# Remainder queries of two heads in two column tiles, whole-block output stores, a new opening and a written-out engine order in a fused attention and maxout kernel

## The chip, the cores and the metric

The kernel runs on one core of one Trainium2 chip. The metric is device time in microseconds (us) of one execution; a "run" below is several executions of one kernel on one chip, with executions of the kernel before among them. The profiled execution of a run has a span that is about 2 us shorter than its time, since the span counts from the first to the last instruction.

Engine names as the profile has them: PE is TensorE (PEld its weight loads), DVE is VectorE, ACT is ScalarE, POOL is GpSimd, SP the engine that issues most transfers. "L582" is line 582 of the kernel in question; the same statement has another line number in another kernel, so lines are named in words too.

## The reference, cut to what matters

```python
q, k, v: (8 batches, 8 heads, 1152, 64)
q_pool = q.reshape(B, H, 576, 2, 64).mean(axis=3)          # 576 queries per head
attn   = softmax(q_pool @ k.T / 8)                          # 576 x 1152
x      = (attn @ v), heads side by side                     # 4608 tokens x 512
out    = maximum(x @ w1, x @ w2) @ w_out                    # 512 -> 1024 -> 512
```

The kernel uses max(a, b) = max(a - b, 0) + b. It therefore makes a hidden layer h = relu(x (w1 - w2)) and an output p = h w_out + x (w2 w_out). Two heads form a pair; there are 32 pairs, four to a batch. Per pair the kernel makes scores, exponentials and attention outputs (AV). Per batch it transposes the outputs (xT) for the hidden layer.

Of the kernel before, what the change touches and what calls it, by code (L numbers as in the profile page):

```python
# [7 lines left out]
P = 128  # L8
# [4 lines left out]
ALU = mybir.AluOpType  # L13


class Plan:
# [29 lines left out]
    def when(self, eng, r=(), w=(), after=()):  # L46

        t = self.free.get(eng, 0.0)
        for d in self.deps(r, w, after)[0]:
            p = self.ops[d]  # L50
            if p["eng"] != eng or p["dma"] is not None:
                t = max(t, p["seen"] + 0.05)
        return t

    def op(self, eng, fn, r=(), w=(), dma=None, cost=0.1, mode="f", after=(), solo=False):
# [9 lines left out]
        if dma is not None:  # L65
            self.free[eng] = t + (1.3 if mode == "t" else 0.5)
            self.dma_free = max(self.free[eng] + 1.2, self.dma_free) + cost
            seen = self.dma_free + 0.7
        else:
            if eng == "PE" and mode != self.mode:  # L70
                t += 0.1
                self.mode = mode
            self.free[eng] = t + cost
            seen = t + cost + self.LAT[eng]
# [8 lines left out]

    def solve(self):
# [3 lines left out]
        for n, o in enumerate(ops):  # L88
# [3 lines left out]
            for d in sorted(o["deps"], reverse=True):  # L92
                p = ops[d]
                if p["dma"] is None:
                    if p["eng"] == eng and (eng == "PE" or d not in o["raw"]):
                        continue
# [57 lines left out]
def bass_funnel_attn__then__act_maxout2_kernel(  # L154
# [32 lines left out]
    with ctx:  # L187
# [10 lines left out]
        qp = [sbuf([HP, QU, 2, D], BF16, f"qp{s}") for s in range(2)]  # L198
# [4 lines left out]
        et = sbuf([P, 4 * PW + HP], BF16, "et")  # L203
        et2 = et[:, 0:4 * PW].rearrange("p (h c) -> p h c", h=2)
# [25 lines left out]

        def setup():
# [5 lines left out]
            def ones(g):  # L237
                g.memset(et[:, 4 * PW:], 0.0)
# [4 lines left out]
            op("POOL", ones, w=["vE0", "vE1", "vE2", "pad"])  # L243

        def load_k(i, lo=0, hi=NT):
            b, h0, s = i // NHP, 2 * (i % NHP), i % 3
            op("SP", lambda e: e.dma_start(
                kraw[s][:, :, lo:hi, :],
                k[b, h0:h0 + 2, :, :].rearrange("h (p t) d -> p h t d", t=NT)[:, :, lo:hi, :]),
                w=[f"kraw{s}"] if hi == NT else [f"kraw{s}.0"], dma=f"d_k{s}" if hi == NT else "d_k",  # L250
                cost=1.5 * (hi - lo) / NT)

        def load_q(i):
            b, h0, s = i // NHP, 2 * (i % NHP), i % 3
            for half in range(2) if i == 0 else (None,):
                at = slice(0, P) if half is None else rows(half)
                hs = slice(h0, h0 + 2) if half is None else slice(h0 + half, h0 + half + 1)
                op("SP", lambda e, at=at, hs=hs: e.dma_start(
                    qraw[s][at, :, :, :].rearrange("p u r d -> p (u r d)"),
                    q[b, hs, :, :].rearrange("h (p r) d -> (h p) (r d)", p=HP)),  # L260
                    w=["qraw0.0"] if half == 0 else [f"qraw{s}"],
                    dma="d_q" if half == 0 else f"d_q{s}", cost=1.45 if half is None else 0.75)
# [8 lines left out]
        def cast_k(i):  # L271
# [4 lines left out]
                w=[f"kbf{s}"] + (["kbf0.0", "kbf0.3"] if i == 2 else []), cost=1.13)  # L276

        def cast_k0(lo, hi, part):
            op("ACT", lambda e: e.activation(
                kbf[0][:, lo:hi, :, :].rearrange("p t h d -> p h t d"), kraw[0][:, :, lo:hi, :],  # L280
                COPY), r=[part], w=[f"kbf0.{lo}"], cost=0.2 + (hi - lo) * 0.092)
# [10 lines left out]

        def cast_q(i):
            s, r = i % 2, i % 3
            for half in range(2):
                a = qraw[r][rows(half), :, :, :]
                op("DVE" if i == 0 else "POOL", lambda g, half=half, a=a: g.tensor_tensor(  # L297
                    qp[s][:, :, half, :], a[:, :, 0, :], a[:, :, 1, :], ALU.add),
                    r=["qraw0.0" if i == 0 and half == 0 else f"qraw{r}"], w=[f"qp{s}.{half}"], cost=0.65 if i == 0 else 1.4,
                    solo=i > 0 and half == 1)  # L300

        def cast_v(i):
# [3 lines left out]
                1.0, 1.0, ALU.mult, ALU.mult), r=[f"vraw{r}"], w=[f"vE{r}"], cost=1.13)  # L306

        def unit(r, cost, go, mode="f"):
# [3 lines left out]
            return r, plan_it, cost  # L312
# [4 lines left out]
        def qtrans(i):  # L317
# [10 lines left out]
            def evac(m):  # L328
                mb = fb[m][:, :].bitcast(BF16)
                dve(lambda e: e.tensor_copy(qpT[i % 3][:, :], mb[:, 0:SQ]),  # L330
                    [f"f{m}"], [f"qpT{i % 3}", f"f{m}"], 0.4)
            return Job("q", [unit([f"qp{s}.0", f"qp{s}.1", "ident"], 0.3, go, "s")], evac, ("q", i))

# [7 lines left out]
        def ktrans_pe(i, cuts=(0, 5, 9)):  # L341
# [3 lines left out]
            for lo, hi in zip(cuts, cuts[1:]):  # L345
# [8 lines left out]
                def evac(m, lo=lo, hi=hi):  # L354
# [4 lines left out]
                        [f"f{m}"], kkeys(i, lo, hi) + [f"f{m}"], 0.1 + (hi - lo) * 0.12)  # L359
# [5 lines left out]
        def av_jobs(i):  # L365
# [5 lines left out]
            need = [f"et{es}.{g - first(i)}" for g in range(first(i), after(i))] + [f"vE{vs}", "pad"]  # L371

            def chunk(half, sb):

                def go(e, m):
                    for t in range(NT):
                        a = (half * 2 + es) * PW + t * SQ + sb * P
# [5 lines left out]

            def norm(half):
                def evac(m):
                    c = c0 + half * D
                    a = fb[m][:, 0:(NCH + 1) * 66].rearrange("p (j c) -> p j c", c=66)
                    dve(lambda e: e.reciprocal(rc[half][:, :], a[:, :, 64:65]),  # L388
                        [f"f{m}"], [f"rc{half}"], 0.19)
                    dve(lambda e: e.tensor_tensor(  # L390
                        xnat[xs][:, :, c:c + D], a[:, :, 0:D],
                        rc[half][:, :].unsqueeze(2).to_broadcast([P, NCH + 1, D]), ALU.mult),
                        [f"f{m}", f"rc{half}"],
                        [f"xn{xs}.{h0 + half}", f"f{m}"], 0.5)
                return evac

            return [Job("a", [chunk(half, sb) for sb in range(NCH + 1)], norm(half), nb=i)
                    for half in range(2)]
# [21 lines left out]
        def skeys(g):  # L420
            return [key for i, t, *_ in pieces(g) for key in (f"kT{i % 3}.{t}", f"qpT{i % 3}")]

        def scores(g):
# [10 lines left out]
            def exp(a, z, keys):  # L434
# [3 lines left out]
                    r=[f"s{r}"], w=keys + [f"s{r}"], cost=0.24 + (z - a) / 700.0)  # L438
# [20 lines left out]
        def under(n0, n1):  # L459

            keys = [key for key, lo, hi in (("w2b", 512, 1536), ("w2T", 1536, 2560),
                                            ("w2f", 2560, NTOK)) if n0 < hi and lo < n1]
            if "w2T" in keys:
                keys += [f"w2T{ct}" for ct in range(NC_)]
            return keys

        def xsize(j):
            return P if j < NCH else NB

        def xtrans(b):  # L470
            xs = b % 2
            assert b == 0 or not queue["w"]
            for j in range(NCH + 1):
# [3 lines left out]
                    r=[f"xn{xs}.{h}" for h in range(H)], w=xkeys(n0, n0 + n),  # L477
                    after=under(n0, n0 + n), dma=f"d_x{xs}{j}", cost=0.65, mode="t")

        def xtrans_pe(b):  # L480
            xs = b % 2
            jobs = []
            for j in range(NCH + 1):
# [14 lines left out]
                jobs.append(Job("x", [unit([f"xn{xs}.{h}" for h in range(H)] + ["ident"],  # L498
# [15 lines left out]
        def w_cast(part, ct):  # L514
            if part == 0:
                dve(lambda e: e.tensor_copy(w2b[:, ct, :], w2f[:, ct, :]),
                    [f"w2f{ct}"], [f"w2b{ct}", "w2b"], 0.6)
            elif part == 1:
                dve(lambda e: e.tensor_tensor(  # L519
                    wd[:, ct, :], w1f[:, ct, :], w2f[:, ct, :], ALU.subtract),  # L520
                    [f"w1f{ct}", f"w2f{ct}"], [f"wd{ct}", "w2f"], 1.2)
            else:
                dve(lambda e: e.tensor_copy(  # L523
                    wo[:, 2 * ct:2 * ct + 2, :], wof[:, 2 * ct:2 * ct + 2, :]),
                    [f"wof{ct}"], [f"wo{2 * ct}", f"wo{2 * ct + 1}"], 0.6)

        def w2t_job(ct):
# [7 lines left out]
            def evac(m):  # L535
# [3 lines left out]
                    [f"f{m}"], [f"w2T{ct}", "w2T", f"f{m}"], 1.15)  # L539
            return Job("w", [unit([f"w2b{ct}", "w2b", "ident"], 0.44, go)], evac)  # L540
# [19 lines left out]
        def store(lo, s):  # L560

            for half in range(2):
                n0 = lo + half * HP
                b, at = n0 // SQ, n0 % SQ
                if b % 2:
                    at = (at - NB) % SQ
                op("SP", lambda e, b=b, u=at // HP, half=half: e.dma_start(
                    out[b * SQ:(b + 1) * SQ, :].rearrange("(p u) e -> u p e", u=QU)[u, :, :],
                    osb[s][rows(half), :]), r=[f"osb{s}"], dma=f"d_o{s}", cost=0.4)
# [4 lines left out]
        def h_jobs(nb, tail):  # L574
# [4 lines left out]
            for ft in range(NF):  # L579
# [6 lines left out]
                def evac(m, ft=ft):  # L586
# [5 lines left out]
                    else:  # L592
                        dve(lambda e: e.tensor_scalar_max(  # L593
                            gT[:, ft, g0:g0 + size], fb[m][:, 0:size], 0.0),
                            [f"f{m}"], w, 0.1 + size / 960.0)
# [3 lines left out]
        def p_job(lo, tail):  # L599
            hi = lo + P  # L600

            def part(j):
                def go(e, m):
# [5 lines left out]
                    return e.matmul(fb[m][:, :], lhs, rhs, start=(j == 0), stop=(j == NC_ + NF - 1))  # L609
                if j < NC_:  # L610
                    return unit([f"w21{j}"] + xkeys(lo, hi), 0.216, go)
                return unit([f"wo{j - NC_}", f"gT.{lo % RING // P}.{j - NC_}"], 0.216, go)

            def evac(m):
                o = ocount[0] % 4
# [6 lines left out]
                else:  # L622
                    dve(lambda e: e.tensor_copy(osb[o][:, :], fb[m][:, :]),  # L623
                        [f"f{m}"], [f"osb{o}", f"f{m}"], 0.63)
                held[o] = (lo, o)
            return Job("p", [part(j) for j in range(NC_ + NF)], evac, nb=hi)
# [11 lines left out]
        p_got = set()  # L638
        p_at = [0]
# [53 lines left out]
        def start_w(n):  # L693
            for ct in range(NC_):
                load("w", (n, ct), got_w, f"{('w2f', 'w1f', 'wof')[n]}{ct}")

        def got_w(at):
# [3 lines left out]
            def ready():  # L701
# [3 lines left out]
                elif n == 2 and ct == NC_ - 1:  # L705
# [18 lines left out]
        def flush():  # L724
# [24 lines left out]
            for b in list(x_wait):  # L749
# [3 lines left out]
                elif plan.ops[plan.writer[f"xn{b % 2}.{H - 1}"]]["seen"] <= now():  # L753
# [15 lines left out]
        def burst_size():  # L769

            done = [b for b in range(B) if all(av_half.get(b * NHP + j) == 2 for j in range(NHP))]
            return 3 if len(done) * SQ - p_end[0] > LAG else 2

        def more_moe():
# [10 lines left out]
            while p_at[0] + P <= h_end[0] and f"w21{NC_ - 1}" in plan.writer:  # L785
                queue["p"].append(p_job(p_at[0], tail))
# [58 lines left out]
        def emit_unit(kk):  # L845
# [17 lines left out]
            elif job.kind == "p":  # L863
                p_got.add(job.nb)
                while p_end[0] + P in p_got:
                    p_end[0] += P
            if job.done:
# [7 lines left out]

        setup()
        load_q(0)
        load_k(0, 0, 3)
        load_k(0, 3, NT)
        cast_k0(0, 3, "kraw0.0")  # L880
        cast_q(0)
        cast_k0(3, NT, "kraw0")
        queue["q"].append(qtrans(0))
        queue["k"].extend(ktrans_pe(0, (0, 3, NT)))
        load_k(1)
        load_q(1)
        load_v(0)
        cast_k(1)
        queue["k"].extend(ktrans_pe(1))
        cast_q(1)  # L890
        queue["q"].append(qtrans(1))
        cast_v(0)
        load("k", 2, load_k, "kraw2")
# [99 lines left out]
```

## The kernel before: what the change and the argument touch

A Python planner with a cost model decides the order of all engines at build time and greedily. Scores come in bursts, because the score matmuls use 64 rows of the array (both heads at once, in two row tiles) and nearly everything else uses 128, and going from one shape to the other costs time (95 to 99 ns in the trace of the kernel before). Each score group of 512 columns for both heads fills one of three buffers of 128x1024 f32 that TensorE writes, and ScalarE turns it into exponentials.

The AV of one head is five chunks of nine matmuls (576 queries are 4.5 blocks of 128, so the fifth chunk is half empty):

```python
def chunk(half, sb):
    def go(e, m):
        for t in range(NT):                                   # NT = 9
            a = (half * 2 + es) * PW + t * SQ + sb * P
            last = e.matmul(fb[m][:, sb * 66:sb * 66 + 65], et[:, a:a + P],
                            vE[vs][:, t, half, 0:65], start=(t == 0), stop=(t == NT - 1))
        return last
    return unit(need, 0.275, go)
...
return [Job("a", [chunk(half, sb) for sb in range(NCH + 1)], norm(half), nb=i) for half in range(2)]
```

An output block of 128 tokens goes out as two transfers of 64 rows. The 64 rows of a half lie 9 rows apart in the output, and the other half fills the rows next to them:

```python
def store(lo, s):
    for half in range(2):
        n0 = lo + half * HP                                   # HP = 64
        b, at = n0 // SQ, n0 % SQ
        if b % 2:
            at = (at - NB) % SQ
        op("SP", lambda e, b=b, u=at // HP, half=half: e.dma_start(
            out[b * SQ:(b + 1) * SQ, :].rearrange("(p u) e -> u p e", u=QU)[u, :, :],
            osb[s][rows(half), :]), r=[f"osb{s}"], dma=f"d_o{s}", cost=0.4)
```

The burst rule and the ranks of the greedy planner:

```python
return 3 if len(done) * SQ - p_end[0] > LAG else 2            # score groups in one burst
rank = {"q": 6, "k": 6, "x": 5, "a": 4, "w": 3, "p": 2, "h": 1}
```

The softmax here doesn't subtract the row's maximum and nothing guards it: scores larger than these inputs give would overflow.

## Time and profile before

The median was 384.99 us (383.74 to 385.46).

The first fence is the profile page of the kernel before: span, busy time by engine (share of the span, number of instructions), and rows of 40 equal slices of the span in tenths. PEclk is the granted TensorE clock.

```profile
span 382.8 us, 11318 instructions
...
PE 363.7 (95%) x5010; PEld 210.8 (55%) x5010; DVE 140.2 (37%) x283; ACT 316.9 (83%) x355; POOL 162.0 (42%) x135
...
PE   2787999999999999999999999999999999999995
...
ACT  3998989999999999999999999999899999902210
...
PEclk9999999999999999999999999999999999999999
...
DMA packets 93521, 88.58 MB, mean 231 GB/s; under 512 B 66080, under 2 KB 66592, under 8 KB 93472
```

The table by windows of the kernel before: for each stretch its length and the busy time (and instructions) of PE, PEld, DVE, ACT and POOL, then clock, DMA share and GB/s.

```profile
80.00:120.00 40.00, 39.94 (x575) 22.50 (x572) 13.10 (x28) 37.66 (x42) 19.92 (x17) 1.00 1.10 268
200.00:240.00 40.00, 40.00 (x584) 23.49 (x583) 13.47 (x28) 37.44 (x43) 18.33 (x16) 1.00 1.11 254
```

TensorE is busy all the time, ScalarE nearly so (37.4 to 37.7 of 40 us), and the last exponential ends at about 335 us while TensorE still has some 45 us of hidden layer and output to do.

I also split TensorE's time by the starts of the matmuls in the trace. "Streaming" is the pace of a dense row of them (29 ns for a 65-column matmul, 216 ns for 512). "Changes" is the extra time, up to 100 ns each (95 to 99 ns where nothing was waited for), where two neighbours use the array in different shapes (64-row transposes count as another shape than the scores; without that it is 261 changes, the prediction's "about 260"). "Waits" is the rest. A second count of this table, with slightly other paces, agrees to about 1 us in each row.

| kernel before, us | |
|---|---|
| before the first matmul | 6.7 |
| streaming | 325.5 |
| changes of shape (277) | 25.1 |
| waits (13.0 of them before 60 us) | 21.0 |
| last matmul's start to the end | 4.5 |

### The profile page before, as it was taken

The numbers are of one execution on the slowest core, as the hardware profiler recorded it, in microseconds if no ns is written. First come the engines' busy times: TensorE is split into PE (matmuls) and PEld (weight loads), VectorE is DVE, ScalarE is ACT, GpSimd is POOL, SyncE is SP. The second block draws the span as 40 slices with busy tenths as digits, with TensorE's granted clock in tenths as the row PEclk, the third lists the DMA queues.
The fourth block names the chain that finished last, engine by engine and source line by source line (L and its number), as shares of the span: only waits on it lengthen the run. The fifth ranks groups of instructions, "written<-read, shape, count | busy, mean of one in ns | idle before, by whom it ended". The sixth has DMA issues, their size and how long they took to land.

```text
span 382.8 us, 11318 instructions
## 1 busy us (share of the span) xinstructions
PE 363.7 (95%) x5010; PEld 210.8 (55%) x5010; DVE 140.2 (37%) x283; ACT 316.9 (83%) x355; POOL 162.0 (42%) x135
## 2 busy tenths in 40 slices
PE   2787999999999999999999999999999999999995
PEld 1365546555555555455556565555455655667642
DVE  2274934442234223422252224422442244237201
ACT  3998989999999999999999999999899999902210
POOL 1955597665554555555453535545545110000000
PEclk9999999999999999999999999999999999999999
DMA  8999999999989998999799999999899460121144
GB/s 248 405 391 399 392 257 312 331 309 312 225 234 295 273 272 174 309 320 275 142 265 289 319 179 212 286 258 315 200 236 267 94 109 14 29 44 42 29 95 98
DMA packets 93521, 88.58 MB, mean 231 GB/s; under 512 B 66080, under 2 KB 66592, under 8 KB 93472
## 3 DMA queue, kind: packets, MB, share of 16 engines
q1 hardware_dynamic: 93472, 87.86, 89.4%
q8 instruction: 39, 0.64, 0.7%
q14 instruction: 10, 0.08, 0.1%
HBM read 62.91 MB, written 9.44 MB: 189 GB/s over the span
## 4 chain that ended last, share of the span: by engine, by line
PE 85%; DMA 6%; DVE 4%; POOL 2%; issue 1%; SPq 1%; POOLq 0%
PE fb L378 22%; PE fb L609 21%; PE sps L429 18%; PE fb L582 15%; PE sps L609 4%; DMA qraw<-in_q_dram 3%; DMA kraw<-in_k_dram 2%; PE sps L582 2%; DVE wd L519 2%; POOL qp L297 1%; PE fb L547 1%; DVE xnat L390 1%; POOL vE L304 1%; PE fb L489 1%; DVE wo L523 1%
## 5 line engine op out<-in xcount | busy, mean ns | idle before, releaser
L436 ACT ACTIVATE et<-sps 128x1024 bf16<-128x1024 f32 (+1 forms) x336 | 307.8, 1005 | 19.0 <-PE sps L429 17.2
L378 PEld LDWEIGHTS fb<-vE,et 128*128 128x128 bf16 x2880 | 93.4, 97 | 20.9 <-issue 10.9
L378 PE MATMUL fb<-vE,et 128*128 128x65 bf16 x2880 | 101.9, 193 | 0.3
L297 POOL TENSOR_TENSOR qp<-qraw 64x576 bf16<-64x576 f32 x62 | 88.6, 1429 | 30.6 <-DMA qpT<-qp 21.3
L429 PE MATMUL sps<-qpT,kT 64*128 64x512 bf16 (+7 forms) x1152 | 96.9, 289 | 3.0 <-ACT et L436 2.1
L304 POOL TENSOR_SCALAR vE<-vraw 128x1152 bf16<-128x1152 f32 x32 | 36.9, 1152 | 103.2 <-PE fb L378 95.8
L429 PEld LDWEIGHTS sps<-qpT,kT 64*128 64x128 bf16 x1152 | 41.8, 95 | 51.3 <-issue 19.6
L582 PE MATMUL fb<-xT,wd 128*128 128x512 bf16 (+3 forms) x276 | 63.1, 360 | 0.7 <-DVE stage L623 0.7
L609 PE MATMUL fb<-wo,stage 128*128 128x512 bf16 x240 | 62.4, 380 | 0.0
L593 DVE TENSOR_SCALAR stage<-fb 128x512 bf16<-128x512 f32 (+3 forms) x64 | 41.9, 657 | 32.3 <-PE fb L582 32.1
L388 DVE RECIPROCAL rc<-fb 128x5 f32<-128x5 f32 x64 | 12.4, 194 | 112.3 <-PE fb L378 112.3
L273 POOL TENSOR_SCALAR kbf<-kraw 128x1152 bf16<-128x1152 f32 x31 | 36.2, 1167 | 14.6 <-DMA kraw<-in_k_dram 12.5
L582 PEld LDWEIGHTS fb<-xT,wd 128*128 128x128 bf16 x276 | 22.8, 98 | 29.4 <-DVE stage L593 6.3
L623 DVE COPY stage<-fb 128x512 f32<-128x512 f32 x29 | 20.0, 690 | 50.2 <-PE fb L609 49.7
L609 PEld LDWEIGHTS fb<-wo,stage 128*128 128x128 bf16 x240 | 21.1, 97 | 23.3 <-issue 3.3
L390 DVE TENSOR_TENSOR xnat<-fb,rc 128x320 bf16<-128x320 f32 x64 | 31.5, 491 | 2.2
L609 PE MATMUL fb<-w,xT 128*128 128x512 bf16 x120 | 32.1, 380 | 0.0
L609 PEld LDWEIGHTS fb<-w,xT 128*128 128x128 bf16 x120 | 10.3, 98 | 11.7 <-issue 2.0
L589 ACT ACTIVATE stage<-sps 128x256 bf16<-128x256 f32 (+1 forms) x7 | 2.3, 338 | 16.4 <-PE sps L582 16.4
L620 ACT COPY stage<-sps 128x512 f32<-128x512 f32 x3 | 1.8, 585 | 13.8 <-PE sps L609 13.8
L609 PE MATMUL sps<-wo,stage 128*128 128x512 bf16 x48 | 11.3, 379 | 0.0
L582 PE MATMUL sps<-xT,wd 128*128 128x256 bf16 (+2 forms) x76 | 10.3, 275 | 0.0
(40 smaller groups left out, 96.4 us busy)
## 6 DMA issues: line engine op xcount, KB each, us to landing
vraw<-in_v_dram SPq DMA_DIRECT2D x32, 576.0 KB, 7.7
kraw<-in_k_dram SPq DMA_DIRECT2D x31, 576.0 KB, 6.6
qraw<-in_q_dram SPq DMA_DIRECT2D x31, 576.0 KB, 5.8
out_dram<-stage SPq DMA_DIRECT2D x72, 128.0 KB, 2.4
xT<-in_moe_w_dram SPq DMA_DIRECT2D x4, 512.0 KB, 11.9
stage<-in_moe_w_out_dram SPq DMA_DIRECT2D x4, 512.0 KB, 14.2
stage<-in_moe_w_dram SPq DMA_DIRECT2D x4, 512.0 KB, 13.2
qraw<-in_q_dram SPq DMA_DIRECT2D x2, 288.0 KB, 4.1
```

What stands on the lines that cost most here:

```text
L273: op("POOL", lambda g: g.tensor_scalar(kbf[s][:, :, :, :].rearrange("p t h d -> p h t d"), kraw[r][:, :, :, :], 1.0, 1.0, ALU.mult, ALU.mu ...
L297: op("DVE" if i == 0 else "POOL", lambda g, half=half, a=a: g.tensor_tensor(qp[s][:, :, half, :], a[:, :, 0, :], a[:, :, 1, :], ALU.add), ...
L304: op("POOL", lambda g: g.tensor_scalar(vE[r][:, :, :, 0:D].rearrange("p t h d -> p h t d"), vraw[r][:, :, :, :], 1.0, 1.0, ALU.mult, ALU.m ...
L378: last = e.matmul(fb[m][:, sb * 66:sb * 66 + 65], et[:, a:a + P], vE[vs][:, t, half, 0:65], start=(t == 0), stop=(t == NT - 1))
L388: dve(lambda e: e.reciprocal(rc[half][:, :], a[:, :, 64:65]), [f"f{m}"], [f"rc{half}"], 0.19)
L390: dve(lambda e: e.tensor_tensor(xnat[xs][:, :, c:c + D], a[:, :, 0:D], rc[half][:, :].unsqueeze(2).to_broadcast([P, NCH + 1, D]), ALU.mult ...
L429: last = e.matmul(sps[r][:, h, col:col + hi - lo], kT[i % 3][rows(h), t, :], qpT[i % 3][rows(h), lo:hi], start=True, stop=True)
L436: op("ACT", lambda e: e.activation(et2[:, :, c:c + z - a], sps[r][:, :, a - g * W:z - g * W], EXP, scale=scale), r=[f"s{r}"], w=keys + [f" ...
L582: return e.matmul(fb[m][:, 0:size], wd[:, ct, ft * P:(ft + 1) * P], xT[:, ct, n0:n1], start=(ct == 0), stop=(ct == NC_ - 1))
L593: dve(lambda e: e.tensor_scalar_max(gT[:, ft, g0:g0 + size], fb[m][:, 0:size], 0.0), [f"f{m}"], w, 0.1 + size / 960.0)
L609: return e.matmul(fb[m][:, :], lhs, rhs, start=(j == 0), stop=(j == NC_ + NF - 1))
L623: dve(lambda e: e.tensor_copy(osb[o][:, :], fb[m][:, :]), [f"f{m}"], [f"osb{o}", f"f{m}"], 0.63)
```

## The change

Its intent: make the half-empty fifth chunks of a pair's two heads in one go, each head in one 64-column tile of the array; start earlier; make longer score bursts; store a block in one transfer; split the last block so that its store starts earlier; and replace the planner's greedy order on TensorE and VectorE by a table that was annealed on a model of the engines. The diff, cut to its core:

```diff
+ORDER = {"PE": ("000210000010110201000110000304400021200010000120011000300000201104...  # cut: 1,471 picks in all
+         "DVE": ("01000110002001100001123111111...                                     # cut
...
+            def rest():
+                def go(e, m):
+                    for t in range(NT):
+                        for half in range(2):
+                            a = col(half, t, NCH)
+                            last = e.matmul(
+                                fb[m][rows(half), NCH * 66:NCH * 66 + 65], et[:, a:a + NB],
+                                vE[vs][:, t, half, 0:65], start=(t == 0), stop=(t == NT - 1))
+                    return last
+                return unit(need, 0.275, go, "c")
...
-            return [Job("a", [chunk(half, sb) for sb in range(NCH + 1)], norm(half), nb=i)
+            return [Job("a", ([] if half else [rest()]) + [chunk(half, sb) for sb in range(NCH)],
...
-            for half in range(2):
-                n0 = lo + half * HP
-                ...
-                    out[b * SQ:(b + 1) * SQ, :].rearrange("(p u) e -> u p e", u=QU)[u, :, :],
-                    osb[s][rows(half), :]), r=[f"osb{s}"], dma=f"d_o{s}", cost=0.4)
+            u = at // HP if b % 2 == 0 else (at - NB) // HP
+            if u == QU - 1:
+                to = out[b * SQ:(b + 2) * SQ, c0:c1].rearrange("(b p u) e -> u b p e", b=2, u=QU)[u]
+            else:
+                to = out[b * SQ:(b + 1) * SQ, c0:c1].rearrange("(p u) e -> u p e", u=QU)[u:u + 2]
+            op(eng, lambda e: e.dma_start(to, osb[s][:, c0:c1]), r=[f"osb{s}"], ...)
...
-            return 3 if len(done) * SQ - p_end[0] > LAG else 2
+            return 3 if done else 2
...
-        rank = {"q": 6, "k": 6, "x": 5, "a": 4, "w": 3, "p": 2, "h": 1}
+        rank = {"q": 6, "k": 6, "x": 5, "h": 5, "a": 4, "w": 3, "p": 1}
...
-            if ready and stall <= 0.1:
+            if ready and stall <= 0.05:
...
+        plan.arrange(ORDER)
         plan.solve()
```

Left out: the opening (q of the first pair in two column parts, k in one transfer and not two, casts in smaller parts), the order of loads, the last output block in parts of 384 and 128 columns, and retuned costs of the planner's model.

## The prediction

> **What bounds it now.** TensorE. The busy summary gives PE 363.7 of 382.8 us, ACT 316.9; from 80 to 320 us the table by windows shows PE busy 39.3 to 40.0 of every 40 us. The last exponential starts at 334.1 us, and about 45 us of matmuls follow, so PE work saved anywhere shortens that tail. Matmul starts in the timeline, taken apart: about 325 us of back-to-back streaming (29 ns per 128x65 matmul, 216 ns per 512-column one), 25 us extra at about 260 changes between 64-row score matmuls and full-array ones (95 to 99 ns each), 21 us of waits, 6.7 us before the first matmul, 4.5 us after the last starts. 13 us of the waits lie in the first 60 us; later it is about 0.5 us in 20.
>
> **What the change does, and its worth on the PE.**
> 1. Remainder queries: per pair of heads 90 matmuls of 128x65 become 72 plus 18 of 64 columns in two column tiles. [...] then the 18 take the time of 9. No run yet shows it for columns; for rows the trace agrees (two heads' score matmuls start 3 to 4 ns apart). Worth 288 x about 30 ns = 8.7 us. [...] One more change per pair: 32 x 0.1 = 3.2 us back. [...] no trace shows what 64-column loads cost. If they don't hide, the step is worth -3 us or worse. I count +4 us.
> 2. Longer score bursts (3 once any batch is finished; now 66 of 3, 55 of 2): some 15 bursts fewer, 0.2 us each: 2.8 us.
> 3. New load order, smaller first casts, rewritten opening, annealed order: of the 13 us of early waits (longest: 1.6 us at 33.6 for a k cast, 1.0 us at 48 for an eviction) and the 6.7 us start I count 5 us; 1 us of later waits. Waits at 10 to 19 us stay: the exponentials (about 0.9 us each) set the pace there.
> 4. Tail: last output block in parts of 384 and 128 columns, on two engines: 0.7 us of the 4.5.
> 5. Costs: two small VectorE multiplies more per pair and more self-waits (DVE is 37% busy, so nearly free). Whole stores halve the store issues (no gain on the path).
>
> Sum: 4 + 2.8 + 6 + 0.7 = 13.5 us, almost all on the chain; I shade it by 1 us for order effects that an engine model gets wrong.
>
> **Prediction: 372.5 us (385.0 before), 8 in 10 between 363 and 381. Faster by over 2%: 0.76; within 2%: 0.20; slower by over 2%: 0.04.**
>
> **What would show it.** (1) The 64-column matmuls start in pairs a few ns apart, 18 take about 0.28 us; with slow loads 0.5 us or more. (2) Score bursts fall to about 120, mode changes stay near 260. (3) First exponential a little before 8.9 us; PE waits before 60 us fall from 13 us to 9. (4) Last matmul to end: 4 us or less. The last exponential ends near 335 and the tail is the shorter part.
>
> **What would make it wrong.** Column-tile loads that serialize (377 or more); an annealed order that fits a model but stalls on the chip, since both engines' orders are fixed and one late operation holds all behind it; or an order better than I credit, removing most waits (365 or less). Late VectorE evictions would show as PE waits on VectorE in the middle.

(4 + 2.8 + 6 + 0.7 = 13.5 us, less the 1 us of shade, takes 385.0 to 372.5 us. The 4 us is 8.7 - 3.2 = 5.5 us, marked down because nothing had measured what the loads for two column tiles cost. That the 18 matmuls take the time of nine was an assumption then; the 3 to 4 ns between the starts of score matmuls in two row tiles was its only measurement.)

## More of the kernel before

The DMA issues of the kernel before: what is moved, how often, KB each, and the median us from issue to landing.

```profile
vraw<-in_v_dram SPq DMA_DIRECT2D x32, 576.0 KB, 7.7
kraw<-in_k_dram SPq DMA_DIRECT2D x31, 576.0 KB, 6.6
qraw<-in_q_dram SPq DMA_DIRECT2D x31, 576.0 KB, 5.8
out_dram<-stage SPq DMA_DIRECT2D x72, 128.0 KB, 2.4
```

## The result and the profile after

The changed kernel took **457.86 us** (454.38 to 459.97, 4 executions) against 385.02 us: ratio 1.188, interval 1.181 to 1.195. It is correct and 19% slower. Ratios here and below are the mean time of one kernel's fast executions over that of the other's of the same rounds, so not quite the ratio of the medians quoted beside them.

The page of the changed kernel, the same lines:

```profile
span 458.2 us, 11357 instructions
...
PE 367.8 (80%) x4981; PEld 210.7 (46%) x5040; DVE 149.1 (33%) x350; ACT 315.0 (69%) x356; POOL 160.8 (35%) x133
...
PE   3889999993698895791998759993994999997940
...
ACT  3999999994498797493598929993886699012200
...
PEclk9999999998799999797799959997998899998995
...
DMA packets 92483, 88.57 MB, mean 193 GB/s; under 512 B 65042, under 2 KB 65298, under 8 KB 92434
```

The busy times have hardly moved (PE 363.7 to 367.8 us, ACT 316.9 to 315.0). What is new is holes: seven or so stretches, from the tenth slice on, where PE and ACT fall together, and where the granted clock falls too. The waits of the changed kernel name them (who waited for whom: us in total, times, longest us):

```profile
ACT et L547 <- PE sps L540: 71.9, 35, 12.8
...
PE fb L694 <- DMA xT<-xnat: 36.4, 5, 11.4
...
PE sps L540 <- DMA kT<-kbf: 12.7, 2, 7.2
```

TensorE waits for transfers: five times for a batch's transposes (L694 is the hidden layer), twice for transposed keys. ScalarE then waits for TensorE. The landing times of the changed kernel's DMA issues say that the loads of k, v and q have become slower, although as many bytes are moved (88.58 and 88.57 MB on the two pages):

```profile
kraw<-in_k_dram SPq DMA_DIRECT2D x32, 576.0 KB, 9.2
vraw<-in_v_dram SPq DMA_DIRECT2D x32, 576.0 KB, 9.6
qraw<-in_q_dram SPq DMA_DIRECT2D x31, 576.0 KB, 9.1
out_dram<-stage SPq DMA_DIRECT2D x35, 256.0 KB
```

(6.6, 7.7 and 5.8 us before. The transposes are slower too, those of k by 8.2 for 6.5 us; the loads of the weights, which are over before the first store, are not: 9.7, 13.1 and 13.3 us, for 11.9, 14.2 and 13.2 before. For the whole stores this list gives no landing time; it is worked out below.) One hole close up, in the timeline of the changed kernel (start us, length us, engine, line, what): first the issuing queue, then TensorE.

```profile
100.54 4.38 SPq L424 DMA_TRANSPOSE qpT<-qp  x1
105.38 3.83 SPq L351 DMA_TRANSPOSE kT<-kbf  x1
109.26 7.41 SPq L588 DMA_TRANSPOSE xT<-xnat  x5
```

```profile
106.44 0.45 PE L469 MATMUL fb<-vE,et 128*128 128x65 bf16 x9
118.32 1.06 PE L694 MATMUL fb<-xT,wd 128*128 128x512 bf16 x2 [11.44 <-DMA xT<-xnat]
```

The five transposes of batch 1 go out from 109.26 us on (from 95.59 us in the kernel before, and from 102.60 us in the changed kernel with half stores below, so that about half of this delay belongs to the new order), behind two other transposes that took 4.38 and 3.83 us to issue, and TensorE stands still for 11.44 us. And near the end, in the chain of the work that ended last, a store alone is on the path for 12.34 us and another for 8.30 us, since an output buffer comes free only when its store has landed; before, the whole stretch from the last matmul's start to the end was 4.5 us.

```profile
402.21 12.34 DMA out_dram<-stage
...
433.68 8.30 DMA out_dram<-stage
```

So the transfers are late, and the one thing about them that the change alters throughout is the store. As the instructions in the traces have it, the old half store writes 64 rows in one dimension ([64,1]). The new whole store writes two neighbouring pooled positions, 64 rows of each ([64,2]), so its pattern in DRAM has an outermost dimension of 2. (A block that spans two batches is different: there the two parts follow each other at the same distance, and the instruction in the trace has one dimension of 128, [128,1].)

The trace shows in two ways what goes with this pattern. The first is the stores' own completion: the trace holds every update that a transfer makes to its semaphore. The blocks that span two batches are a control that the change itself contains, a whole store of the same 256 KB with another outermost dimension:

```
store                                         number   updates each   us from issue to landing, median (range)
before, a pair of half stores of 64 rows          36       2 x 16        2.4  (2.4 to 7.3)
changed, whole, outermost dimension 2             31            3        9.7  (7.7 to 18.6)
changed, whole, one dimension of 128               4           16        6.2  (2.3 to 8.1)
```

(Two smaller stores of the last block, left out of the table, have 3 updates too.) Of the 3 updates, one comes 0.9 to 5.3 us after the issue (median 1.0) and two at the store's end (median 20 ns apart). The four control stores have 16. One of them landed in 2.3 us, and no store with an outermost 2 in under 7.7 us; the other three took 4.5 to 8.1 us, with other transfers under way. So the number of updates goes with the outermost dimension, and not with the store's being whole.

The second way is the packets. Output rows are packets of 2,048 bytes (4,608 of the 5,632 packets of that size before; 4,480 in the changed kernel, whose last block goes out in narrower rows), and the 64 KB store of the last block has the only packets of 512 bytes:

```
                                  before    changed    changed, half stores
2,048-byte packets                 5,632      5,632      5,632
  median us of one                 0.095      0.084      0.089
  time with any in flight, us       59.8      188.9       62.7
  mean number in flight             11.7        2.7       10.4
512-byte packets, most in flight      -          2         15
```

After 60 us, when nearly all packets of that size are output rows, exactly two are in flight for 153.6 of the 177.0 us with any. Before, 16 is the number in flight for longest (16.4 of 52.7 us). An estimate from these numbers: 32 of the 36 blocks, 4,096 rows, two at a time are 2,048 x 0.084 = 172 us, where the 4,608 rows before, 16 at a time, are 288 x 0.095 = 27 us.

What lies behind a store is held up meanwhile, as the hole above shows: there store packets are in flight from 103.7 to 108.7 us, two at a time, and 16 packets of the transpose of the queries that start between 103.6 and 104.4 us all end at about 110.4 us, each in flight for 6.1 to 6.8 us. After 60 us the median packet of a transpose takes 18 ns in all of these kernels; the longest takes 9.7 us in the changed kernel, 3.2 us before, and 2.2 us in the changed kernel with half stores. Which engine a packet ran on the trace does not say.

### The profile page after: what moved, and what is told of

It is laid out like the page before. It is cut to its first block, busy times and chain, and to the rows that moved or that the text cites. A ratio compares the mean times of both kernels' runs of the same rounds, so it can differ in the third digit from the quotient of the medians.

```text
span 458.2 us, 11357 instructions
## 1 busy us (share of the span) xinstructions
PE 367.8 (80%) x4981; PEld 210.7 (46%) x5040; DVE 149.1 (33%) x350; ACT 315.0 (69%) x356; POOL 160.8 (35%) x133
## 2 busy tenths in 40 slices
DMA packets 92483, 88.57 MB, mean 193 GB/s; under 512 B 65042, under 2 KB 65298, under 8 KB 92434
## 4 chain that ended last, share of the span: by engine, by line
PE 50%; DMA 19%; ACT 12%; SPq 11%; DVE 2%; issue 2%; POOL 1%; POOLq 0%
ACT et L547 12%; PE sps L540 12%; PE fb L721 11%; PE fb L694 11%; PE fb L469 10%; SPq L588 6%; DMA out_dram<-stage 5%; DMA xT<-xnat 4%; DMA kT<-kbf 4%; SPq L351 4%; PE sps L694 2%; DMA kraw<-in_k_dram 2%; DMA qraw<-in_q_dram 2%; PE fb L481 2%; DMA vraw<-in_v_dram 2%
## 5 line engine op out<-in xcount | busy, mean ns | idle before, releaser
L540 PE MATMUL sps<-qpT,kT 64*128 64x256 bf16 (+7 forms) x1152 | 100.0, 291 | 18.1 <-DMA kT<-kbf 12.7
L694 PE MATMUL fb<-xT,wd 128*128 128x512 bf16 (+2 forms) x244 | 63.5, 395 | 37.6 <-DMA xT<-xnat 36.4
L469 PE MATMUL fb<-vE,et 128*128 128x65 bf16 x2232 | 85.0, 193 | 2.5 <-issue 1.9
L469 PEld LDWEIGHTS fb<-vE,et 128*128 128x128 bf16 x2232 | 76.3, 97 | 17.4 <-issue 6.7
L705 DVE TENSOR_SCALAR stage<-fb 128x512 bf16<-128x512 f32 (+2 forms) x60 | 39.9, 671 | 96.3 <-PE fb L694 88.7
L694 PEld LDWEIGHTS fb<-xT,wd 128*128 128x128 bf16 x264 | 24.1, 104 | 64.1 <-issue 46.6
L491 DVE RECIPROCAL rc<-fb 128x5 f32<-128x5 f32 (+1 forms) x62 | 11.6, 187 | 81.8 <-PE fb L469 81.5
L501 DVE TENSOR_TENSOR xnat<-fb,rc 128x256 bf16<-128x256 f32 x62 | 26.2, 424 | 2.1
L750 ACT COPY stage<-sps 128x512 f32<-128x512 f32 x3 | 1.8, 586 | 26.2 <-PE sps L721 26.2
L721 PE MATMUL sps<-wo,stage 128*128 128x512 bf16 (+2 forms) x71 | 15.3, 355 | 0.1
L481 PE MATMUL fb<-vE,et 128*64 128x65 bf16 x558 | 14.7, 197 | 0.2 <-ACT et L547 0.2
L481 PEld LDWEIGHTS fb<-vE,et 128*64 128x64 bf16 x558 | 11.3, 111 | 7.6 <-issue 6.5
## 6 DMA issues: line engine op xcount, KB each, us to landing
stage<-in_moe_w_out_dram SPq DMA_DIRECT2D x4, 512.0 KB, 13.1
stage<-in_moe_w_dram SPq DMA_DIRECT2D x4, 512.0 KB, 13.3
```

What stands on the lines that cost most here:

```text
L481: last = e.matmul(fb[m][rows(half), NCH * 66:NCH * 66 + 65], et[:, a:a + NB], vE[vs][:, t, half, 0:65], start=(t == 0), stop=(t == NT - 1))
L501: dve(lambda e: e.tensor_tensor(xnat[xs][:, 0:NCH, c:c + D], a[:, 0:NCH, 0:D], rc[half][:, 0:NCH].unsqueeze(2).to_broadcast([P, NCH, D]), ...
L540: last = e.matmul(sps[r][:, h, col:col + hi - lo], kT[i % 3][rows(h), t, :], qpT[i % 3][rows(h), lo:hi], start=True, stop=True)
L694: return e.matmul(fb[m][:, 0:size], wd[:, ct, ft * P:(ft + 1) * P], xT[:, ct, n0:n1], start=(ct == 0), stop=(ct == NC_ - 1))
L705: dve(lambda e: e.tensor_scalar_max(gT[:, ft, g0:g0 + size], fb[m][:, 0:size], 0.0), [f"f{m}"], w, 0.16 + size / 960.0)
L721: return e.matmul(fb[m][:, 0:c1 - c0], lhs, rhs[:, c0:c1], start=(j == 0), stop=(j == NC_ + NF - 1))
```

## The experiments

I name two theories first. **Theory A**: a whole store with an outermost dimension of 2, whose packets go two at a time in the trace above, holds up everything behind it. **Rival B**: the written-out order is at fault, since it holds all work behind one late operation. A second rival, **C**, is the new load order and VectorE's additional waits for itself.

### Half stores put back into the changed kernel

```diff
-            op(eng, lambda e: e.dma_start(to, osb[s][:, c0:c1]), r=[f"osb{s}"], ...)
+            op(eng, lambda e: [e.dma_start(to[half], osb[s][rows(half), c0:c1]) for half in range(2)],
+               r=[f"osb{s}"], ..., parts=2)       # one planned operation, two transfers
```

> The changed kernel, with only its output stores put back to two transfers of 64 rows each; the table order on TensorE and VectorE is untouched. Theory A (a whole store, whose output pattern has 2 as its outermost dimension, [...] holds up every later transfer): the long waits go, 365 to 375 us, clock back to 1.00, landing of k, q, v loads back to about 6 to 8 us. Rival B (the fixed order waits for late operations): still above 430 us. Rival C (new load order or the VectorE self-waits): still above 430 us.

Measured: 383.68 us against 384.36 (ratio 0.997, interval 0.995 to 0.999). The order of TensorE, VectorE and GpSimd is instruction for instruction that of the changed kernel. From its page and its DMA issues:

```profile
span 382.3 us, 11394 instructions
...
PEclk9999999999989999999999999999999999999999
...
kraw<-in_k_dram SPq DMA_DIRECT2D x32, 576.0 KB, 6.9
vraw<-in_v_dram SPq DMA_DIRECT2D x32, 576.0 KB, 7.7
qraw<-in_q_dram SPq DMA_DIRECT2D x31, 576.0 KB, 6.0
out_dram<-stage SPq DMA_DIRECT2D x70, 128.0 KB, 2.5
```

Landing times are back to those of before and 74 us are gone: theory A holds, and rivals B and C, which expected more than 430 us, fall. But the number that I expected, 365 to 375 us, was missed as well. That is a second question, taken up below.

### Whole stores alone, in the kernel before

```diff
-            for half in range(2): ... (two transfers of 64 rows)
+            to = ... [u:u + 2]   (or "u b p e" [u])              # as in the change
+            op("SP", lambda e: [], ..., parts=0)                  # keeps the plan as it was
+            op("SP", lambda e: e.dma_start(to, osb[s][:, :]), ...)
```

> The kernel before, with only its stores changed to whole 128-row transfers as in the change; every engine's order otherwise the same. Theory A: 430 to 470 us, with long waits of TensorE for transposes and loads. Rivals B and C: within 1% of 385 us.

Measured: 461.72 us against 384.36 (ratio 1.200). The order of the computing engines is that of the kernel before. Its waits, again who waited for whom:

```profile
ACT et L437 <- PE sps L430: 75.0, 61, 14.8
...
PE fb L583 <- DMA xT<-xnat: 34.7, 5, 13.1
```

and the landing of its loads:

```profile
vraw<-in_v_dram SPq DMA_DIRECT2D x32, 576.0 KB, 9.7
kraw<-in_k_dram SPq DMA_DIRECT2D x31, 576.0 KB, 8.1
qraw<-in_q_dram SPq DMA_DIRECT2D x31, 576.0 KB, 9.0
```

This one edit makes the whole slowdown, with the same signature (36.4 us of waits for xT in the changed kernel, 34.7 here). Its stores show the same split as above: 32 of 36 with 3 updates and 9.7 us to landing, four with 16 updates. Rivals B and C are not needed for it.

### The changed kernel without its table

```diff
-        plan.arrange(ORDER)
```

> The changed kernel with whole stores, but without the table: the order that the planner itself makes. Theory A: still above 430 us. Rival B (the table is the cause): 365 to 390 us.

Measured: 456.04 us (ratio 1.186). The table is not the cause.

### Half stores, without the table

> Half stores and the planner's own order. Theory A: 367 to 380 us; what it lies above the run with half stores and the table is the worth of the table, which I put at 2 to 6 us. Rival B: clearly faster than the run with half stores and the table.

Measured: 386.89 us (ratio 1.005, interval 1.003 to 1.007). The time itself, expected at 367 to 380 us, was missed again. The table is worth 386.89 - 383.68 = 3.2 us, within the 2 to 6 us that I had put. It is a gain, but it repairs what something else had lost.

### Where did the other 12 us go? The same split of TensorE's time

The page of the changed kernel with half stores counts 5,040 weight loads but 4,981 matmuls, so 59 matmul records are missing. I counted a gap of 195 to 235 ns as one missing 512-column matmul. Two later runs with the same work and no missing record gave 318.0 and 318.3 us of streaming, which agrees with 318.2 here. (The other columns but the first have the same correction for 50 to 53 missing records.) The correction is good to 1 or 2 us, and so are the differences between columns: a recount finds 47 such gaps for the 51 missing records of the tiles alone (0.9 us of streaming too little), and some 60 for the 50 of the run without the table, some of them matmuls at half clock (2 us of streaming that belong to its waits).

| us | before | changed, half stores | tiles alone in before | half stores, no table | the same, old ranks and bursts |
|---|---|---|---|---|---|
| before the first matmul | 6.7 | 4.4 | 6.8 | 4.4 | 4.3 |
| streaming | 325.5 | 318.2 | 317.1 | 320.3 | 318.5 |
| changes of shape (number) | 25.1 (277) | 29.6 (321) | 29.3 (315) | 28.2 (300) | 28.6 (303) |
| waits | 21.0 | 26.2 | 28.0 | 29.6 | 26.0 |
| of them before 60 us | 13.0 | 14.1 | 14.7 | 12.8 | 13.7 |
| last matmul to the end | 4.5 | 3.8 | 4.5 | 3.8 | 3.7 |
| span | 382.8 | 382.3 | 385.7 | 386.3 | 381.2 |

The column tiles do save streaming time (7.3 us in the second column). Changes of shape (4.5 us) and waits (5.2 us) take it back. The next experiments ask why.

### The tiles alone, in the kernel before

The edit is the `rest` job of the diff above with its normalization, put into the kernel before with nothing else of the change.

> The kernel before with the column tiles for the remainder queries alone (its own planner, its own half stores). Theory T (tiles save 288 matmul times of 30 ns and cost one mode change of 0.1 us per pair): 379 to 382 us, 1 to 1.5% below before. Rival (the tiles' gain is eaten by mode changes and by work coming at other times, as the run with half stores and the table suggests): 384 to 387 us.

Measured: 388.05 us against 384.27 (ratio 1.010, interval 1.006 to 1.013). Theory T missed: it is 1% slower, and above the rival's range too. By the table the tiles gave 8.4 us of streaming as intended (about 7.5 with the four gaps that weren't found), cost 4.2 us of changes, and waits rose by 7.0 us (6.1 with the same correction). The greedy planner makes another order with the tiles; that the waits come from it is likely but not tested.

### Neighbouring matmuls in the same tile

```diff
-                    for t in range(NT):
-                        for half in range(2):
+                    for half in range(2):
+                        for t in range(NT):
```

> The changed kernel with half stores and table, but the 18 remainder matmuls of a pair in another order: nine of one head, then nine of the other, so that neighbours share a column tile. Theory T (neighbours in different column tiles run at once): 18 take 0.52 us in place of 0.28, 32 x 0.25 = 8 us more on TensorE, so 389 to 392 us. Rival (the overlap is not on the path): within 1 us of the run with half stores, 383.7 us.

Measured: 387.67 us (ratio 1.008, interval 1.004 to 1.012), 4.0 us above the run with half stores and the table. The same 18 matmuls in the timeline of that run, and then in this one:

```profile
107.08 0.47 PE L482 MATMUL fb<-vE,et 128*64 128x65 bf16 x18
```

```profile
107.77 0.66 PE L482 MATMUL fb<-vE,et 128*64 128x65 bf16 x18
```

From the first start to the last the 18 take 281 ns against 463 ns (medians of the 32 groups). With the heads alternating, two matmuls start 2 to 5 ns apart, and the next two about 30 ns after. So matmuls in different column tiles overlap here, and the tiles work. Without the overlap the time was below the 389 to 392 us that theory T expected, since the 18 take 0.46 and not 0.52 us; 32 x 0.18 = 5.8 us of TensorE work came back as 4.0 us of time.

### The first load of k in two transfers again

> The changed kernel with half stores and table, and the first load of k again in two transfers (three of nine row groups first). Theory O (the new opening made the first exponential late, 10.8 us in place of 8.9, and the exponentials lead until about 60 us): first exponential at about 9 us and 1 to 2 us less in all, 382 us. Rival (the late start is absorbed): 383.7 us.

The changed opening did not start the exponentials earlier. In the timelines, first of the kernel before and then of the changed kernel with half stores, the first exponentials are:

```profile
8.91 3.77 ACT L436 ACTIVATE et<-sps 128x1024 bf16<-128x1024 f32 x4 [0.61 <-PE sps L429]
```

```profile
10.82 10.19 ACT L548 ACTIVATE et<-sps 128x1024 bf16<-128x1024 f32 x11 [2.02 <-PE sps L541]
```

In the edited kernel the first exponential still started at 10.44 us, so the edit didn't do what it was meant to; the time was 384.2 us (ratio 0.999). The other ten profiled executions with the changed opening had it at 7.6 to 11.0 us (median 9.7), the six with the old one at 8.6 to 9.2 (median 9.0), so it varies. This experiment is inconclusive on what an early start is worth. The new opening brought none in the median.

### The old ranks and the old burst rule

```diff
-        plan.arrange(ORDER)
-            return 3 if done else 2
+            return 3 if len(done) * SQ - p_end[0] > LAG else 2
-            if ready and stall <= 0.05:
+            if ready and stall <= 0.1:
-        rank = {"q": 6, "k": 6, "x": 5, "h": 5, "a": 4, "w": 3, "p": 1}
+        rank = {"q": 6, "k": 6, "x": 5, "a": 4, "w": 3, "p": 2, "h": 1}
```

(in the changed kernel with half stores)

> The changed kernel with half stores, without the table, and with the planner's old ranks of work and old burst rule. Theory R (the new ranks and the tighter burst rule delay the attention outputs of batch 1, so its transposes and the hidden layer behind them come late): the 4 us wait of TensorE near 108 us goes and the time is 380 to 383 us, against 386.9 us with the new ranks and no table. Rival: no change, 386 to 388 us.

Measured: 383.35 us (ratio 0.997, interval 0.995 to 0.998), 3.5 us below the run without the table and with the new ranks, a little above the 380 to 383 us that theory R expected, and as fast as the run with the table. The wait near 108 us is gone. The new ranks and burst rule had thus cost about what the table gave. (The three settings were changed together; I can't say which of them it was.)

### The wait near 108 us

In the changed kernel with half stores, one wait stands out in the timeline of TensorE:

```profile
112.64 1.48 PE L695 MATMUL fb<-xT,wd 128*128 128x512 bf16 x3 [4.17 <-DMA xT<-xnat]
```

The attention outputs of batch 1 were done at 102.6 us (95.0 before), so their transposes were issued at 102.6 (95.6 before) and the hidden layer behind them waited. To take that wait away without touching the order, the hidden layer of tokens 512 to 1023 reads other, earlier tokens (wrong):

```diff
-                                        xT[:, ct, n0:n1], ...
+                                        xT[:, ct, 0:size] if nb == 1 else xT[:, ct, n0:n1], ...
```

> The changed kernel with half stores and table, wrong on purpose: the hidden layer of tokens 512 to 1023 reads the tokens 0 to 511, so it needs none of batch 1's transposes; order and amount of work are the same. Theory W (the 4.3 us wait near 108 us is a loss on the path that the fixed order makes): 3.5 to 4.3 us less, 379 to 380.5 us. Rival (the wait only moves, since the exponentials hold TensorE there): within 1 us of 383.7 us.

Measured: 383.16 us (ratio 0.996, interval 0.993 to 1.000; executions from 381.85 to 385.74). The wait went away. In the profiled execution, the slowest of the six (385.74 us), another came 36 us later, for the transposes of the next batch:

```profile
149.45 1.87 PE L696 MATMUL fb<-xT,wd 128*128 128x512 bf16 x4 [4.91 <-DMA xT<-xnat]
```

By the median the rival was right (0.5 us below the run with the wait), and this trace shows where the wait moved to. It need not move so in every execution: the fastest took 381.85 us at a clock of 1.000, and it was not profiled. That TensorE had caught up with what the exponentials and the transposes deliver fits, but is not shown. This wait has a second cost: the four matmuls of that line start 380 to 427 ns apart and not 216, and the trace has the granted clock at half from 147.6 to 154.4 us. The wait was 5.1 us long from start to start (144.4 to 149.5 us); the half clock lasted 6.8 us, 4.9 us of them after the wait had ended. In the changed kernel's trace a half clock goes with each of seven waits of 3.1 to 11.6 us and ends 2.3 to 5.9 us after the wait; in the kernel before, where no two starts are over 2 us apart, the mean clock was 1.000. A half clock also came without one long wait: in the run with long bursts below, at 108.2 us, after four gaps of 0.8 to 0.9 us between matmul starts within 3.6 us (36 matmuls from 108.34 us on took 2.16 us, and 1.26 us at 102.76).

### Longer bursts

```diff
+                least = 3 if size == 3 and cand else 1
-                while size > 1 and (not ready or stall > 0.05):
+                while size > least and (not ready or stall > 0.05):
```

(in the run with old ranks, with bursts of three asked for once a batch is done, and then from the 30th group on)

> The changed kernel with half stores, no table, old ranks, and bursts of three score groups kept to once a batch is done (116 bursts by count, 131 in the run with old ranks and bursts, 383.35 us). Theory S (TensorE is the limit, and each burst fewer saves two mode changes of 0.1 us): 2 to 3 us less, 380 to 381.5 us, last exponential later. Rival (longer bursts starve ScalarE and that costs as much): 383 to 385 us.

> As the run with long bursts, but bursts of three from the 30th score group on (114 bursts, 97 of three). Theory S: within 1 us of the run with long bursts, no worse. Rival: slower than it by 1 us or more, since the exponentials lead before 60 us.

Measured: 385.19 us (ratio 1.000) and 389.49 us (ratio 1.011). Theory S fell both times. In the first, changes of shape did fall from 303 to 275 (2.7 us), but waits rose from 26.0 to 31.4 us; in the second, 271 and 36.0. In the first, part of the new waits are TensorE's for score buffers, as the weight loads of the score matmuls show; first the run with old ranks, then the two with long bursts:

```profile
PEld sps L541 <- ACT et L548: 36.5, 106, 1.0
```

```profile
PEld sps L541 <- ACT et L548: 40.2, 109, 1.0
```

```profile
PEld sps L541 <- ACT et L548: 29.2, 90, 1.0
```

In the second that wait fell. There, by my recount, most of the new waits lie before the hidden layer's matmuls (7.2 us in place of 0.4); why is not shown.

### TensorE work taken away in a fixed order

The forecast had assumed that TensorE work saved anywhere shortens the run. Here it is tested by itself in the kernel before, with no change of shape added: of nine remainder matmuls only the first is made. Their outputs are wrong, which doesn't matter for the times. The work taken away is an estimate from the 29.5 ns or so of one such matmul.

```diff
+                    some = range(1) if sb == NCH and half == 1 else range(NT)     # one head, all pairs
+                    # or: sb == NCH and i < 9 ; sb == NCH and i >= 20
-                    for t in range(NT):
+                    for t in some:
```

> The kernel before, wrong on purpose: of one head's nine remainder matmuls in each pair only the first is made; order, bursts and all else the same. It takes 32 x 8 x 29.5 ns = 7.6 us of TensorE work away, about what the column tiles do, without a mode change. The forecast's step (work saved anywhere counts): 7 to 7.6 us less, 377 us. Theory P (before about 110 us the exponentials and the transposes pace TensorE, so only the savings of pairs after the ninth count): 4.5 to 6 us less, 379 us.

> The same for both heads but in pairs 0 to 8 alone (their outputs are made before about 113 us): 9 x 16 x 29.5 ns = 4.2 us of TensorE work less. The forecast's step: 4 us less, 380.5 us. Theory P: less than 1 us.

> The same for both heads in pairs 20 to 31 alone (after about 225 us): 12 x 16 x 29.5 ns = 5.7 us of TensorE work less. Both the forecast's step and theory P: 5 to 5.7 us less, 379 us.

| | TensorE work less, us | measured, median us | ratio (interval) | ratio as us | share that came back |
|---|---|---|---|---|---|
| all pairs, one head | 7.6 | 380.12 | 0.988 (0.985 to 0.992) | 4.5 | 0.6 |
| pairs 0 to 8 | 4.2 | 382.43 | 0.994 (0.992 to 0.996) | 2.4 | 0.6 |
| pairs 20 to 31 | 5.7 | 383.12 | 0.996 (0.993 to 0.998) | 1.7 | 0.3 |

(Ratio as us is one minus the ratio, times 385.0.) The forecast's step fell in all three. My theory P met the first, at the lower edge of its 4.5 to 6 us, and fell in the other two: early savings are not lost altogether and late ones don't count in full. Between a third and two thirds of what is saved comes back; with the intervals, that is 0.4 to 0.8 in the first two and 0.1 to 0.5 in the third. The waits of the kernel before and then of the run with short late pairs show where some of the rest goes (score matmuls' weight loads waiting for the exponentials that free their buffer):

```profile
PEld sps L429 <- ACT et L436: 15.3, 37, 0.8
```

```profile
PEld sps L430 <- ACT et L437: 21.8, 55, 1.0
```

Between 220 and 340 us alone this wait rose from 2.8 us (8 times) to 8.6 us (25 times). The bursts stand at fixed places in TensorE's order, at about ScalarE's pace. With less work between them, TensorE comes to the next burst before its buffer is free. In the run with short early pairs the same wait did not rise (14.8 us); there the waits before 60 us rose from 13.0 to 14.3 us.

### The best version

> The run with half stores, no table, old ranks and old burst rule, but once that rule asks for bursts of three they are not cut to two (124 bursts by count, 131 without). If mode changes count after about 110 us: 0.7 to 1.4 us below that run, 382 to 382.7 us, the best so far. Otherwise 383 to 384 us.

Measured: 383.27 us against 385.00 (ratio 0.996, interval 0.994 to 0.997), so the second branch: fewer mode changes brought nothing that can be seen. This is the changed kernel with half stores, no table, old ranks and rules, with three-group bursts not cut once the old rule asks for them. It beats both kernels, the one before by 0.4%, and cannot be told from the run without the last edit (0.997, interval 0.995 to 0.998).

## Why the prediction was wrong

I predicted 372.5 us (363 to 381) and it was 457.86.

- **The step that failed, by far the largest: "Whole stores halve the store issues (no gain on the path)".** I costed the store by the number of issues and not by how its pattern is carried out: 32 of 36 blocks went out two packets at a time and took 9.7 us to land in place of 2.4 (medians), and TensorE waited for transposes held up behind them. Measured alone it costs 461.72 - 384.36 = 77 us in the kernel before, and taking it out of the changed kernel gives 74 us back. I took it for a clean-up, though no trace had shown such a store yet. "What would make it wrong" did not name it either.
- **Column tiles ("I count +4 us"): right in mechanism and in the size on TensorE.** The 18 matmuls take 281 ns to the last start, as predicted (0.28 us). Streaming fell by 7.3 us; that it is not 8.7 fits the 281 ns, to which the pace of nine full-array matmuls (29 ns each) compares as 232 ns to the last start, 1.6 us over 32 pairs. That difference isn't explained here. One more change per pair costs about 3.2 us.
- **"Longer score bursts ... 2.8 us": wrong.** The changed order has 63 bursts of three and 58 of two (66 and 55 before) and 16 of one (7). The planner alone would have made 77 of three; the table cut them up again. Beyond the 32 added changes there are 12 more, so this term cost about 1 us. And the two runs that forced longer bursts showed that they bring nothing here.
- **"New load order, smaller first casts, rewritten opening, annealed order ... 6 us": wrong, in sign too.** With half stores, the time before the first matmul fell by 2.3 us, the waits before 60 us rose by 1.1 us and the later ones by 4.1 us. The exponentials did not start earlier. The table was worth 3.2 us, but the new ranks and burst rule had lost 3.5 us first.
- **"Tail ... 0.7 us": right without the stores' trouble** (4.5 to 3.8 us).
- **"PE work saved anywhere shortens that tail": half right.** Taken away in a fixed order, 30 to 60% of it came back as time. TensorE's 95% busy share hid that ScalarE was busy for 94% of the middle. The longer waits of score loads for exponentials in the run with short late pairs fit that a gain on one engine soon turns into a wait for the other; the run with short early pairs does not show it.

What stays open: why the greedy order with the tiles alone has 6 to 7 us more waits, which of the three planner settings lost the 3.5 us, and what an earlier start of the exponentials would be worth.

## What to carry to other kernels

Before two transfers are merged into one, look at the outermost dimension of the pattern that results: here a merged store with 2 outermost had two packets in flight at a time and took 9.7 us to land in place of 2.4, and the whole kernel slowed by 19 to 20% although the bytes were the same. The list of transfers gave such stores no landing time, and TensorE's waits named other transfers, so look also at later landings by kind, at the number of packets in flight and at how many updates a transfer makes to its semaphore. In this kernel, where two engines are both above 90% busy in an order fixed at build time, only 0.3 to 0.6 of what was saved on one of them came back: count on part of it, and re-plan the order only against measured runs.
